# Which engine signals between score products, and the order of the first period, in an attention and MLP kernel

## The chip, the cores and the metric

The kernel runs on one core of one Trainium2 chip. The metric is the device time of one execution in microseconds (us), from the first to the last thing the device does for it; lower is better. Engines are named as in the profile: PE is TensorE (PEld its weight loads), DVE VectorE, ACT ScalarE, POOL GpSimd, SP SyncE. A name with a q behind it (SPq) is the instruction queue of that engine, which issues DMAs and handles semaphores in program order.

## The reference

Attention over 8 batches of 8 heads, 576 tokens and 64 dimensions, in which only scores within tau of their row's maximum keep a weight; its output, 4608 rows of 512, goes through two matrices with a leaky ReLU between them.

```python
scores = scale * np.matmul(q, k.transpose(0, 1, 3, 2))            # (8, 8, 576, 576)
thresh = np.max(scores, axis=-1, keepdims=True) - tau
scores = np.where(scores >= thresh, scores, -1e9)
scores = scores - np.max(scores, axis=-1, keepdims=True)
attn = np.exp(scores)
attn = attn / (np.sum(attn, axis=-1, keepdims=True) + 1e-09)
x = np.matmul(attn, v).transpose(0, 2, 1, 3).reshape(4608, 512)
h = x @ w_in                                                       # 512 x 2048
return np.maximum(0.01 * h, h) @ w_out                             # 2048 x 512
```

## The kernel before

The work is cut into 72 periods. A period holds 128 queries of four heads; the heads form two pairs, and the two heads of a pair are the two halves (h = 0 and 1) of the 128 rows of PE. So a period has four score tiles (c, h) of 128 x 576, with c the pair. The order of work in a period is written out by hand (the pools do no scheduling), and every engine runs its instructions in that order.

In each period `scores` issues 24 products into `sc`, a PSUM tile of five banks (L296). q and k are each split in two 16-bit parts, a high and a low one, so every piece of a tile takes three products: high with high, low q with high k, high q with low k. The two row halves run beside each other on PE. The four tiles lie in `sc` without gaps, each spans a bank's edge, and tiles of different halves share a bank. So the first product of piece a12 (half 0) must come behind the last product of piece b12 (half 1) of the same period. This order is made by a signal: an instruction without work (`nop`, L325) on another engine waits for b12, and PE waits for the signal ahead of a12. Before the change the signal is on ACT in periods 0 to 2, on POOL in 3 to 5 and on SP from period 6 on. As each queue runs in order, the signal also waits for what stands ahead of it in that queue, and holds up what stands behind it.

DVE then copies each tile out of PSUM with its row's minimum of the negated score (`copy_min`, L332), makes the threshold (L347), and multiplies the exponentials that ACT computes (L358) by the mask (L369), which gives the weights w; ACT does one or two of the tiles by itself (L363, L364). In periods 0 to 2 PE transposes the weights (L388, copied by ACT and DVE, L393); from period 3 on SP issues a DMA transpose into wT (`turn_w`, L380). Two periods later PE multiplies wT with v (`pv`, L417), DVE scales the result (L436), and layer 1 (L457, with ACT's L460) and layer 2 (L470) follow, spread over the periods.

Keys and queries come in by DMA and have to be transposed and split. For batch 0, and a few pieces of batch 1, PE transposes them in 32 bits (`turn32`, L211), ACT takes the high half (`take_high`, L232) and DVE the low half (`take_low`, L239). For the others POOL splits them (L160, L167, L171) and PE transposes both halves (L186). `k32[p]` are the keys of pair p of batch 0, `q32` its queries. Matmuls on a blank tile (`idle`, L514) fill PE in the first four periods.

The queues carry, beside the signals: SP the loads of q, k and v (L75, L86, L99, and L93, L106 for the tails of 64 tokens), the DMA transposes and the stores; POOL the splits, casts of v (L113), the loads of w_in and w_out (L123, L127, cast on the way), copies of the first keys (L253), and from period 5 on the loads of tails.

In period 0 PE's order is: the products of both pairs, the transposes of `k32[2]` and `q32[1, 0]`, 32 idle products, the transposes of `k32[3]`; then period 1. DVE's is: `take_low` of `k32[1]` (ahead of the loop), the copies of tiles 0, 1 and 2, `take_low` of `k32[2]`, the copy of tile 3, `take_low` of `q32[1, 0]`, the threshold, weights. The products of the second pair need the low half of `k32[1]`.

Of the kernel before, what the change touches and what calls it, by code (L numbers as in the profile page):

```python
# [33 lines left out]
def kernel(  # L34
# [10 lines left out]
    nc = tc.nc  # L45
# [128 lines left out]
    def turn(keys):  # L174

        banks = [ps.tile([128, 1024], FP16, tag="h", bufs=2, name="tp") for _ in range(2)][::-1]
        at_ = 0
        for key in keys:
            half, n = halves.pop(key), tokens(key)
            tps[key] = [t[:, ds(at_, 128 * n)].rearrange("d (x t p) -> d x t p", x=2, t=n) for t in banks]  # L180
            at_ += 128 * n
            for x in range(2):
                for t in range(n):
                    for r in range(2):
                        rows = ds(64 * r, 64)
                        nc.tensor.transpose(tps[key][r][:, x, t, :], half[rows, x, t, :, :].rearrange("p h d -> p (h d)"),  # L186
                                            ident[rows, rows])
        return banks[0]


    def unit32(b, which, p0, np=1, t0=0, nt=4):
        return (b, which, p0, np, t0, nt)
# [3 lines left out]
    def turn32(keys, tag="h"):  # L196
        bank = ps.tile([128, 512], FP32, tag=tag, bufs=2 if tag == "h" else 1, name="tp")
        c0 = 0
        for key in keys:
            b, which, p0, np, t0, nt = key  # L200
            n = 256 if p0 == "t" else 128 * np * nt
            tps32[key] = bank[:, ds(c0, n)]
            if p0 == "t":
                for t in range(2):
                    nc.tensor.transpose(bank[:, ds(c0 + 128 * t, 128)],
                                        tails[b, which][:, t, :, :].rearrange("p h d -> p (h d)"), ident32[:, :])
            else:
                for p in range(np):
                    for t in range(nt):
                        src = raws[b, (p0 + p) // 2, which][:, t0 + t, ds(2 * ((p0 + p) % 2), 2), :]  # L210
                        nc.tensor.transpose(bank[:, ds(c0 + 128 * (nt * p + t), 128)],  # L211
                                            src.rearrange("p h d -> p (h d)"), ident32[:, :])
            c0 += n

    def place32(key, x, i, parts):

        b, which, p0, np, t0, nt = key
        dst, tp = turned_of(b, which), tps32[key]
        if p0 == "t":
            c0 = MAIN if which == "q" else 0  # L220
            return dst[:, x, :, ds(c0, 64)].rearrange("d (u s) p -> d s u p", u=2)[:, i, :, :], \
                tp.rearrange("d (i u p) -> d i u p", i=2, p=64)[:, i, :, :]
        c0 = (64 if which == "k" else 0) + 128 * t0
        n = 128 * nt // parts
        return dst[:, x, ds(p0, np), ds(c0 + n * i, n)], \
            tp.rearrange("d (p c) -> d p c", p=np)[:, :, ds(n * i, n)]

    def take_high(keys, parts=1):
        for key in keys:
            for i in range(2 if key[2] == "t" else parts):  # L230
                dst, tp = place32(key, 0, i, parts)
                nc.scalar.activation(out=dst, in_=tp, func=AF.Copy, bias=0.0, scale=64.0)  # L232

    def take_low(keys, parts=1):
        for key in keys:
            for i in range(2 if key[2] == "t" else parts):
                dst, tp = place32(key, 1, i, parts)
                high, _ = place32(key, 0, i, parts)
                nc.vector.scalar_tensor_tensor(out=dst, in0=tp, scalar=64.0, in1=high, op0=AX.mult, op1=AX.subtract)  # L239
# [34 lines left out]
    def pieces(c, h):  # L274
        a = PLACE[c, h]
        cut = (a // 512 + 1) * 512
        return [(a, cut - a), (cut, a + 576 - cut)]

    HALVES = ((0, 0), (1, 0), (0, 1))

    BEHIND = mybir.DependencyInfo(mybir.DependencyClass.Sync, mybir.DependencyReason.DATA)

    def product(st, c, h, piece, i):
        a, n = piece
        qx, kx = HALVES[i]
        rows = ds(64 * h, 64)
        key0 = 64 * (1 - h) + a - PLACE[c, h]
        for u in range(2 if st.tail else 1):
            pair = 2 * c + u if st.tail else 2 * st.pp + c
            if st.tail:  # L290
                lhs = turned[st.b, "q"][rows, qx, pair, MAIN:S]
                o = sc[ds(64 * u, 64), ds(a, n)]
            else:
                lhs = turned[st.b, "q"][rows, qx, pair, ts(st.m, 128)]
                o = sc[:, ds(a, n)]
            yield nc.tensor.matmul(out=o, lhsT=lhs, rhs=turned[st.b, "k"][rows, kx, pair, ds(key0, n)],  # L296
                                   start=(i == 0), stop=(i == 2), skip_group_check=True)

    TILES = ((0, 0), (0, 1), (1, 0), (1, 1))

    def scores(st):

        st.mn = sb.tile([128, 4], FP32, tag="mn", bufs=2, name="mn")
        st.th = sb.tile([128, 4], FP32, tag="th", bufs=2, name="th")
        st.s, st.e = {}, {}
        (a00, a01), (b01, b00) = pieces(0, 0), pieces(0, 1)
        (a11, a12), (b12, b11) = pieces(1, 0), pieces(1, 1)
        todo = [[(0, a00), (0, a01), (1, a11), (1, a12)], [(1, b12), (1, b11), (0, b01), (0, b00)]]
        if st.n < 2:

            todo[1] = todo[1][2:] + todo[1][:2]
        todo = [[(c, x, i) for c, x in row for i in range(3)] for row in todo]
        at_, signal, first = [0, 0], None, None
        while todo[0] or todo[1]:
            h = 1 if not todo[0] or (todo[1] and at_[1] < at_[0]) else 0
            c, x, i = todo[h].pop(0)
            at_[h] += x[1]
            for mm in product(st, c, h, x, i):
                if first is not None:
                    tc.declare_no_dep(mm.ins, first.ins, reason="other banks")  # L320
                if (h, x) == (0, a12) and i == 0:
                    tc.add_manual_dep(mm.ins, signal.ins.name, BEHIND, reason="the row halves share a bank")
                last = mm
            if (h, x) == (1, b12) and i == 2:
                signal = (nc.scalar if st.n < 3 else nc.gpsimd if st.n < 6 else nc.sync).nop()  # L325
                tc.add_manual_dep(signal.ins, last.ins.name, BEHIND, reason="the row halves share a bank")
            if (h, x) == (0, a11) and i == 2:
                first = copy_min(st, 0)

    def copy_min(st, n):  # L330
        st.s[TILES[n]] = sb.tile([128, 576], FP32, tag=f"s{n}", bufs=1, name="s")
        return nc.vector.tensor_scalar(  # L332
            out=st.s[TILES[n]][:, :], in0=sc[:, ds(PLACE[TILES[n]], 576)], scalar1=-1.0 / UNIT, scalar2=None,
            op0=AX.mult, op1=AX.min, accum_out=st.mn[:, n : n + 1])

    def copies(st, before, taken, lows):
        taken()
        copy_min(st, 1)
        copy_min(st, 2)
        if lows:  # L340
            take_low(lows[0])
        copy_min(st, 3)
        for keys in lows[1:]:
            take_low(keys)
        if before:
            recip(before)
        nc.vector.tensor_scalar(out=st.th[:, :], in0=st.mn[:, :], scalar1=1.0, scalar2=tau_f, op0=AX.mult, op1=AX.add)  # L347
        st.w = sb.tile([128, 2, 9, 128], FP16, tag="w", bufs=3, name="w")
        st.sum = sb.tile([128, 2, 2], FP32, tag="sum", bufs=3, name="sum")
# [23 lines left out]
    def recip(st):  # L373
        st.rec = sb.tile([128, 2, 2], FP16, tag="rec", bufs=4, name="rec")
        with nc.allow_low_precision(reason="as the weights"):
            nc.vector.reciprocal(out=st.rec[:, :, :], in_=st.sum[:, :, :])
# [172 lines left out]
    k32 = [[unit32(0, "k", p)] for p in range(NP)]  # L549
# [13 lines left out]
    take_low([q32[0, 0]])  # L563
    turn32(k32[1], "o")
    take_high(k32[1])
    take_low(k32[1])
    early32[0] = [k32[2], [q32[1, 0]]]
    late32[0] = k32[3]
    early32[1] = [[q32[0, 1]]]
# [46 lines left out]
    n = 0  # L616
    while n < N + PV_LAG or l1q or pending or l2q or stores:
        st = periods[n] if n < N else None
# [4 lines left out]
        keys, now32, late = turns_at.get(n, []), early32.get(n, []), late32.get(n)  # L623


        if st:
            scores(st)
        bank = turn(keys) if keys else None
        for x in now32:
            turn32(x)  # L630
        if here:
            before.wt = sb.tile([128, 2, 9, 128], FP16, tag="wT", bufs=4, name="wT")
# [13 lines left out]
        if st:  # L646
            copies(st, before, lambda: [take(key, 1, on_dve) for key in keys], now32)
            exp_plain(st, 0)
        elif before:
            recip(before)  # L650
# [117 lines left out]
```

## Time and profile before

| | |
|---|---|
| Median of 3 runs | 486.68 us (486.44 to 487.24) |
| The profiled execution | 486.76 us |
| Its span, first to last instruction | 485.0 us |
| PE busy | 467.4 us, 96% of the span |
| DVE, ACT, POOL busy | 433.0, 419.5, 214.9 us |
| Mean granted clock of PE | 0.991 |

Times in the views are microseconds from the start of the span. A row of the timeline gives the start, the time covered, the engine, the line, the operation with its output and inputs, their shapes and the count; in brackets stand the idle time of the engine before it and what ended that. In a row of waits stand the waiting engine and line, whom it waited for, the total, how often, and the longest. In a row of a DMA queue stand packets, MB and the share of 16 engines' time; in a row of DMA issues the count, the KB of each and the time from issue to landing. The chain of waits follows the work back from the last instruction, and shows the piece of each step that counts.

### The profile page before, as it was taken

To read this page: it belongs to the slowest core of one execution; us is meant where nothing else is said; L and a number is where in the kernel's file an instruction comes from. 1 tells how busy PE (TensorE), PEld (TensorE's weight loads), DVE (VectorE), ACT (ScalarE), POOL (GpSimd) and SP (SyncE) were. 2 spreads that over 40 slices of the span, in tenths; PEclk is the share of its full clock that TensorE was granted. 3 is DMA by queue.
4 is the path that set the end of the run, shared out by engine and by line. 5 is a ranking of instruction groups with operands and counts; after the bars stand their busy time and mean duration, and the time that the engine had idled before them with its cause. 6 is when DMAs were issued, how large, how long until landed. Compare 5 with 4: busy or idle time off the path is not lost.

```text
span 485.0 us, 25242 instructions
## 1 busy us (share of the span) xinstructions
PE 467.4 (96%) x10858; PEld 379.5 (78%) x10858; DVE 433.0 (89%) x1313; ACT 419.5 (86%) x779; POOL 214.9 (44%) x353
## 2 busy tenths in 40 slices
PE   8779799999999999999999999999999999999996
PEld 5567688887888888887888888888888788777774
DVE  4988599999999999999999999999999999999940
ACT  3888588998999999999899999999999899988862
POOL 2645545554465574454456574455357464000000
PEclk9999799999999999999999999999999999999999
DMA  9999959699999989799799979698799979557851
GB/s 179 240 209 228 181 146 186 145 163 200 170 198 201 216 151 197 156 167 210 177 185 194 222 164 177 159 182 194 182 188 205 204 173 123 123 122 122 122 96 45
DMA packets 206752, 83.68 MB, mean 173 GB/s; under 512 B 175792, under 2 KB 201392, under 8 KB 206640
## 3 DMA queue, kind: packets, MB, share of 16 engines
q1 hardware_dynamic: 199728, 74.79, 79.1%
q0 software_dynamic: 5504, 6.82, 7.5%
q8 instruction: 85, 1.39, 1.2%
q10 hardware_dynamic: 1408, 0.46, 0.4%
q14 instruction: 27, 0.22, 0.1%
HBM read 36.70 MB, written 9.44 MB: 95 GB/s over the span
## 4 chain that ended last, share of the span: by engine, by line
PE 83%; DMA 6%; ACT 5%; DVE 2%; SPq 2%; issue 1%; ACTq 0%; DVEq 0%
PE hp L457 25%; PE o L470 24%; PE sc L296 20%; PE pv L417 8%; DMA wT<-w 5%; PE tp L401 3%; PE tp L186 3%; ACT e L358 1%; ACT wT L393 1%; SPq L86 1%; DMA raw<-in_k_dram 1%; ACT s L363 1%; DVE w L369 1%; ACT w L364 1%; ACT g L460 1%
## 5 line engine op out<-in xcount | busy, mean ns | idle before, releaser
L332 DVE TENSOR_SCALAR_CACHE_REDUCE s<-sc 128x576 f32<-128x576 f32 x288 | 205.4, 753 | 16.0 <-PE sc L296 15.7
L457 PEld LDWEIGHTS <-win 128*64 128x64 f16 x4608 | 147.1, 111 | 28.9 <-DVE xt L428 1.1
L369 DVE SCALAR_TENSOR_TENSOR w<-s,th,e 128x576 f16<-128x576 f32 x215 | 165.2, 814 | 0.4
L358 ACT ACTIVATE e<-s,mn 128x576 f16<-128x576 f32 x215 | 158.9, 777 | 0.0
L470 PE MATMUL o<-wout,g 128*64 128x512 f16 x1152 | 149.5, 381 | 0.0
L457 PE MATMUL hp<-x,win 128*64 128x128 f16 x4096 | 137.1, 220 | 0.3 <-DVE kT L249 0.3
L296 PE MATMUL sc<-kT,qT 64*128 64x384 f16 (+7 forms) x1920 | 120.7, 284 | 5.1 <-SPq L325 3.4
L460 ACT ACTIVATE g<-hp 128x512 f16<-128x512 f32 x144 | 86.1, 598 | 42.2 <-PE hp L457 42.2
L296 PEld LDWEIGHTS <-qT 64*128 64x128 f16 (+1 forms) x1920 | 90.0, 97 | 22.1 <-SPq L325 4.4
L160 POOL TENSOR_SCALAR scaled<-raw 128x512 f32<-128x512 f32 x53 | 32.7, 616 | 148.8 <-DVE w L369 139.0
L470 PEld LDWEIGHTS <-g 128*64 128x64 f16 x1152 | 58.6, 111 | 29.2 <-issue 0.5
L171 POOL TENSOR_TENSOR half<-scaled,half 128x512 f16<-128x512 f32 (+1 forms) x68 | 71.6, 1053 | 5.8
L364 ACT ACTIVATE w<-s,minus_tau 128x576 f16<-128x576 f32 x73 | 56.6, 775 | 2.4
L363 ACT ACTIVATE s<-s,th 128x576 f32<-128x576 f32 x73 | 56.0, 767 | 0.0
L417 PE MATMUL pv<-wT,v 128*64 128x128 f16 (+1 forms) x1600 | 53.5, 216 | 2.0 <-DMA wT<-w 1.1
L417 PEld LDWEIGHTS <-v 128*64 128x64 f16 x1600 | 46.1, 111 | 3.2 <-issue 1.4
L167 POOL CAST half<-scaled 128x512 f16<-128x512 f32 (+1 forms) x68 | 38.3, 563 | 4.4
L436 DVE TENSOR_TENSOR x<-pv,by 128x256 f16<-128x256 f32 x64 | 27.1, 423 | 8.8 <-PE pv L417 7.6
L407 ACT COPY by<-tp 128x256 f16<-128x256 f16 x72 | 26.8, 372 | 2.3 <-PE tp L388 2.3
L186 PEld LDWEIGHTS <-half 64*128 64x128 f16 x968 | 24.7, 96 | 2.3 <-issue 1.5
L186 PE MATMUL tp<-ident,half 64*128 64x64 f16 x968 | 24.5, 191 | 0.0
L113 POOL CAST v<-vraw 128x256 f16<-128x256 f32 x64 | 24.0, 408 | 0.0
(61 smaller groups left out, 336.8 us busy)
## 6 DMA issues: line engine op xcount, KB each, us to landing
vraw<-in_v_dram SPq DMA_DIRECT2D x16, 512.0 KB, 5.1
out_dram<-osb SPq DMA_DIRECT2D x31, 256.0 KB, 4.0
raw<-in_q_dram SPq DMA_DIRECT2D x13, 512.0 KB, 4.7
raw<-in_k_dram SPq DMA_DIRECT2D x13, 512.0 KB, 4.9
win<-in_moe_w_in_dram POOLq DMA_DIRECT2D x4, 512.0 KB, 11.5
wout<-in_moe_w_out_dram POOLq DMA_DIRECT2D x4, 512.0 KB, 15.0
raw<-in_q_dram SPq DMA_DIRECT2D x12, 128.0 KB, 3.9
raw<-in_k_dram SPq DMA_DIRECT2D x10, 128.0 KB, 4.1
```

Source lines behind the costliest of these rows:

```text
L171: nc.gpsimd.tensor_tensor(out=halves[key][:, 1, 0:n, :, :], in0=scaled.pop(key)[:, 0:n, :, :], in1=halves[key][:, 0, 0:n, :, :], op=AX.sub ...
L186: nc.tensor.transpose(tps[key][r][:, x, t, :], half[rows, x, t, :, :].rearrange("p h d -> p (h d)"), ident[rows, rows])
L296: yield nc.tensor.matmul(out=o, lhsT=lhs, rhs=turned[st.b, "k"][rows, kx, pair, ds(key0, n)], start=(i == 0), stop=(i == 2), skip_group_ch ...
L332: return nc.vector.tensor_scalar(out=st.s[TILES[n]][:, :], in0=sc[:, ds(PLACE[TILES[n]], 576)], scalar1=-1.0 / UNIT, scalar2=None, op0=AX. ...
L358: nc.scalar.activation(out=st.e[t][:, :], in_=st.s[t][:, :], func=AF.Exp, bias=st.mn[:, n : n + 1], scale=-1.0)
L363: nc.scalar.activation(out=z, in_=z, func=AF.Prelu, bias=st.th[:, n : n + 1], scale=-1.0, alpha=1e20)
L364: nc.scalar.activation(out=w_of(st, t), in_=z, func=AF.Exp, bias=minus_tau[:, :], scale=1.0, accum_out=st.sum[:, c, h : h + 1])
L369: st.last = nc.vector.scalar_tensor_tensor(out=w_of(st, t), in0=st.s[t][:, :], scalar=st.th[:, n : n + 1], in1=st.e[t][:, :], op0=AX.is_le ...
L417: nc.tensor.matmul(out=st.pv[ds(64 * h, 64), c, ts(u, n)], lhsT=v16[st.b % 2][:, pair, blk, :], rhs=st.wt[:, c, blk - (blk > 4), ts(u, n)] ...
L457: nc.tensor.matmul(out=hp[ds(64 * c, 64), jj, :], lhsT=w_in16[:, i, ds(128 * (4 * u + jj) + 64 * c, 64)], rhs=g.x[:, i, :], start=(i == 0) ...
L460: nc.scalar.activation(out=g.g[:, ds(4 * u, 4), :], in_=hp[:, :, :], func=AF.Prelu, bias=0.0, scale=1.0, alpha=0.01)
L470: nc.tensor.matmul(out=g.o[ds(64 * c, 64), :], lhsT=g.g[:, j, ds(64 * c, 64)], rhs=w_out16[:, j, :], start=(j == 0), stop=(j == 15), skip_ ...
```

## The change

It does two things. The signal of each period moves to another engine, by a list: POOL in period 0, ACT in 1, SP in 2, POOL in 3 to 8, SP from 9 on. So it changes in periods 0 and 2 (ACT before) and 6 to 8 (SP before).

And period 0 gets another order. All 12 products of pair 0 are issued first; then, before any product of pair 1, come the copies of tiles 0 and 1, `take_low` of `k32[1]` and the 32-bit transposes of `k32[2]` and `q32[1, 0]`. Then pair 1's 12 products follow, and `take_low` of `k32[2]` stands ahead of the copies of tiles 2 and 3. In the other periods the first copy is declared independent of the products issued after it; in period 0 this declaration falls away with the moved copy.

```diff
+    SIGNAL = [nc.gpsimd, nc.scalar, nc.sync] + [nc.gpsimd] * 6 + [nc.sync]
...
-    def scores(st):
+    def scores(st, between=None):
...
         while todo[0] or todo[1]:
+            if between and todo[0][0][0] == 1 and todo[1][0][0] == 1:
+                between()
+                between = None
             h = 1 if not todo[0] or (todo[1] and at_[1] < at_[0]) else 0
+            if between and todo[h][0][0] == 1:
+                h = 1 - h
             c, x, i = todo[h].pop(0)
...
-                signal = (nc.scalar if st.n < 3 else nc.gpsimd if st.n < 6 else nc.sync).nop()
+                signal = SIGNAL[min(st.n, 9)].nop()
                 tc.add_manual_dep(signal.ins, last.ins.name, BEHIND, reason="the row halves share a bank")
-            if (h, x) == (0, a11) and i == 2:
+            if (h, x) == (0, a11) and i == 2 and st.n:
                 first = copy_min(st, 0)
...
     def copies(st, before, taken, lows):
         taken()
-        copy_min(st, 1)
-        copy_min(st, 2)
+        if st.n:
+            copy_min(st, 1)
+            copy_min(st, 2)
         if lows:
             take_low(lows[0])
+        if not st.n:
+            copy_min(st, 2)
         copy_min(st, 3)
...
     take_high(k32[1])
-    take_low(k32[1])
...
-        if st:
+        if n == 0:
+            def between():
+                copy_min(st, 0)
+                copy_min(st, 1)
+                take_low(k32[1])
+                for x in now32:
+                    turn32(x)
+            scores(st, between)
+        elif st:
             scores(st)
         bank = turn(keys) if keys else None
-        for x in now32:
+        for x in now32 if n else []:
             turn32(x)
```

## The prediction

> **What bounds the kernel now.** I read the page first, busy time by engine:
>
> ```profile
> PE 467.4 (96%) x10858; PEld 379.5 (78%) x10858; DVE 433.0 (89%) x1313; ACT 419.5 (86%) x779; POOL 214.9 (44%) x353
> ```
>
> TensorE (PE) is busy for 96% of the span, so the span falls only by PE idle time, or by PE time at a low clock. Then the waits, for idle time that ends in a score signal. From 48 to 75 us:
>
> ```profile
> PE sc L296 <- SPq L325: 2.8, 1, 2.8
> ```
>
> One stall of PE, released by SyncE's queue (SPq) at L325, the score signal. The timeline of PE puts it in period 6:
>
> ```profile
> 50.08 1.32 PE L296 MATMUL sc<-kT,qT 64*128 64x384 f16 x19
> ```
>
> ```profile
> 54.19 0.82 PE L296 MATMUL sc<-kT,qT 64*128 64x256 f16 x5 [2.79 <-SPq L325]
> ```
>
> PE stops at 51.40 with 5 of 24 products left. The timeline of SP's queue shows why the signal is late:
>
> ```profile
> 47.80 3.33 SPq L380 DMA_TRANSPOSE wT<-w  x1
> 51.18 2.89 SPq L86 DMA_DIRECT2D raw<-in_q_dram  x4
> 54.33 3.37 SPq L380 DMA_TRANSPOSE wT<-w  x1
> ```
>
> The signal stands behind the transpose of period 4's weights (47.80) and four loads (51.18 to 54.07). It does no work; SP just isn't there. The stall also costs clock. Two stages of the windows view (length, busy time of PE, PEld, DVE, ACT, POOL, then the granted clock):
>
> ```profile
> 53.00:54.00 1.00, 0.00 (x0) 0.00 (x0) 0.00 (x0) 0.00 (x0) 0.92 (x2) 0.66 0.24 46
> ```
>
> ```profile
> 60.00:60.20 0.20, 0.20 (x10) 0.20 (x8) 0.00 (x0) 0.20 (x2) 0.07 (x1) 0.65 0.25 62
> ```
>
> If the clock is 1.0 or 0.5, a mean of 0.66 over 1 us puts the drop at 53.32 and 0.65 over 0.2 us puts the return at 60.06. So from 54.19 to 60.06 PE works at half rate: 5.87 us, half of it lost, 2.9 us. Stall and slow stretch together are 5.7 us, the most that this place can give.
>
> The other limit here is the transposed weights wT that the second product (pv, L417) reads two periods later:
>
> ```profile
> 38.12 5.93 SPq L380 DMA_TRANSPOSE wT<-w  x1
> ```
>
> ```profile
> 47.64 0.75 PE L417 MATMUL pv<-wT,v 128*64 128x128 f16 x20 [0.45 <-DMA wT<-w]
> ```
>
> wT of period 3 is issued at 38.12, and PE already waits 0.45 us for it at 47.64. The DMA view says what holds it. From 38 to 40 us, then from 42 to 44:
>
> ```profile
> q0 software_dynamic: 409, 0.41, 122.6%
> ```
>
> ```profile
> q1 hardware_dynamic: 749, 0.19, 99.2%
> q0 software_dynamic: 100, 0.09, 27.8%
> ```
>
> While q0 (GpSimd's weight loads) has work, q1 (SP's) moves nothing of the transpose; it moves as q0 drains. So this landing follows the end of the weight loads rather than the compute, and so does SP, whose issue takes 5.93 us here against 3.33 and 3.37 later.
>
> **Period 0.** Pair 0's 12 products stand in the same place. PE rows:
>
> ```profile
> 7.90 1.32 PE L296 MATMUL sc<-kT,qT 64*128 64x384 f16 x16
> 9.38 0.87 PE L296 MATMUL sc<-kT,qT 64*128 64x256 f16 x8 [0.16 <-DVE kT L239]
> 10.18 0.88 PE L211 MATMUL tp<-ident,raw 128*128 128x128 f32 x6
> 10.98 1.94 PE L514 MATMUL spare<-blank,ident 128*64 128x256 f16 x32
> 12.85 0.66 PE L211 MATMUL tp<-ident,raw 128*128 128x128 f32 x4
> ```
>
> Chain of waits, the take_low of k32[1] and the three copies (each with its accumulator):
>
> ```profile
> 8.63 0.70 DVE kT L239
> ```
>
> ```profile
> 9.73 2.12 DVE s L332 x6
> ```
>
> 12 of the 16 products take 12/16 of 1.32 = 0.99 us, so pair 0 ends at 8.89. Now two copies start at 8.92 instead of 9.73, at 2.12/3 = 0.71 each: they end at 10.34. That is a lead of 0.81 us. But in the built program PE's first product of pair 1 waits for the second copy, since nothing declares them independent any more; before, four of pair 1's products ran before any copy. PE fills the gap with the six transposes (0.88, 8.89 to 9.77) and waits to 10.38. Behind the copies stands take_low of k32[1], 10.34 to 11.04; the last eight products need it, 0.87 more: they end at 11.95, not 10.25. The 32 idle products queue behind them: they start at 11.95 instead of 10.98, and all that follows on PE is 0.97 later, the transposes of k32[3] at 13.82 too. From there ACT's and DVE's rows:
>
> ```profile
> 13.62 0.59 ACT L232 ACTIVATE kT<-tp 128x512 f16<-128x512 f32 x1
> ```
>
> ```profile
> 14.39 0.69 DVE L239 SCALAR_TENSOR_TENSOR kT<-tp,kT 128x512 f16<-128x512 f32 x1
> ```
>
> ACT's take_high goes from 13.62 to 13.82 + 0.66 + 0.02 = 14.50, DVE's take_low from 14.39 to 14.50 + 0.59 + 0.03 = 15.12. DVE's weights stand behind it: period 0 ends 0.7 us later, not earlier. From the other side, if pair 1 started as soon as pair 0 ended, about 0.8 us would be won, the lead of the first copy. I take +0.7, since the wait is there. The signal costs nothing: GpSimd's (POOL's) queue holds only the weight loads behind it, which wait for a load of v anyway.
>
> **Period 2.** The signal goes from ACT to SP. PE and ACT rows:
>
> ```profile
> 23.05 0.50 PE L296 MATMUL sc<-kT,qT 64*128 64x256 f16 x5 [1.12 <-ACTq L325]
> ```
>
> ```profile
> 22.98 0.78 ACT L364 ACTIVATE w<-s,minus_tau 128x576 f16<-128x576 f32 x1
> ```
>
> ```profile
> 23.99 0.50 PE L388 MATMUL tp<-ident,w 128*64 128x128 f16 x12
> ```
>
> The 1.12 us wait goes, but L388 transposes what this L364 writes, ready at 23.76 at the earliest: 0.23 us is all that can be won, and 0.1 is what I count. On SP the wait has a queue behind it:
>
> ```profile
> 16.88 1.06 SPq L75 DMA_DIRECT2D raw<-in_q_dram  x1
> 17.98 1.34 SPq L93 DMA_DIRECT2D rawt<-in_k_dram  x2
> ```
>
> ```profile
> raw<-in_q_dram SPq DMA_DIRECT2D x1, 512.0 KB, 10.4
> ```
>
> These loads (640 KB) now issue at about 22.7 to 25 instead of 16.88 to 19.32. With the same 10.4 us the first lands near 33; its reader:
>
> ```profile
> 38.15 0.62 POOL L160 TENSOR_SCALAR scaled<-raw 128x512 f32<-128x512 f32 x1 [3.72 <-PE sc L296]
> ```
>
> So 5 us of cover remain. The bytes move from one part of a full DMA stretch to another, so I leave the end of q0 where it is. If that is wrong, they lengthen it by 640 KB at 0.41 MB in 2 us = 3.1 us (third rival).
>
> **To period 6.** PE reaches pv of period 3 0.6 to 0.7 us later, at 47.19 + 0.7 = 47.89 instead of waiting to 47.64: 0.25 us lost, the rest is eaten by the 0.45 us wait. Scores of period 6 start at 50.33.
>
> **Periods 6 to 8.** POOL's queue at that time:
>
> ```profile
> 47.68 0.67 POOL L171 TENSOR_TENSOR half<-scaled,half 128x256 f16<-128x256 f32 x1
> ```
>
> It is free from 48.35 (+0.7) and its next work waits for DVE, so the 2.79 us stall goes, and with it the half clock. Undisturbed, period 7 shows how long PE needs:
>
> ```profile
> 62.07 1.64 PE L296 MATMUL sc<-kT,qT 64*128 64x384 f16 x24
> 63.55 0.40 PE L186 MATMUL tp<-ident,half 64*128 64x64 f16 x16
> ```
>
> ```profile
> 65.86 0.66 PE L211 MATMUL tp<-ident,raw 128*128 128x128 f32 x4
> 66.62 0.75 PE L417 MATMUL pv<-wT,v 128*64 128x128 f16 x20
> 67.18 0.63 PE L470 MATMUL o<-wout,g 128*64 128x512 f16 x4
> ```
>
> From the scores to the end of layer 1: 65.86 - 62.07 = 3.79, and 0.20 for the 8 more transposes of period 6 (half of 0.40). PE is ready for pv of period 4 at 50.33 + 3.99 = 54.32. What is late next is wT of period 4, issued at 47.80. Its time to landing, in the DMA view:
>
> ```profile
> wT<-w SPq DMA_TRANSPOSE x1, 7.6
> ```
>
> It lands at 55.40, so PE waits 1.1 us, pv runs at 55.44 and layer 2 follows 67.18 - 66.62 = 0.56 later, at 56.00. Before:
>
> ```profile
> 59.20 1.18 PE L417 MATMUL pv<-wT,v 128*64 128x128 f16 x20
> 60.21 0.60 PE L470 MATMUL o<-wout,g 128*64 128x512 f16 x4
> ```
>
> 60.21 - 56.00 = 4.2 us. The next wT, if it takes as long, lands at 54.33 + 7.6 = 61.9, ahead of its pv at 66.62 - 4.2 = 62.4. From there PE is busy nearly throughout, so the lead stays. In periods 7 and 8 SP's signal stalled nobody, so POOL can only lose. Its worst place is period 7:
>
> ```profile
> 57.52 2.55 POOL L93 DMA_DIRECT2D rawt<-in_q_dram  x4
> ```
>
> These four issues end at 60.07; they hang on period 6's transposes, which move some 3 us ahead, so they end near 57 to 58, while the signal is wanted about 1.2 us after the scores of period 7 start at 57.8. I count 0, at worst 1 us.
>
> **Sum.** 0.25 us are lost by period 5, 5.7 us go in period 6, and 1.1 us of new wait come in, which by the start times of layer 2 leaves 4.2 (the three would leave 4.35; pv at half rate and its follower differ by the rest). The profiled execution took 486.76 us, of which 1.8 lie around the span, where nothing changes; the median is 486.68. Less 4.2: 482.5.
>
> **A rule weighed.** The clock fell here after 51.40 to 53.32, 1.9 us without a matmul, in a gap of 2.79 us; the 1.12 us gap at 22 us left it whole. My new gap (54.32 to 55.44) is like the latter, so I charge no clock. The Trainium skill (TensorE: Matmul & The Clock Gate, section "Why this matters for your kernels") allows idle gaps up to about 3 us; by that rule the 2.79 us gap would not have dropped the clock, and the sum by it would be the fourth rival's, 485.5. The trace speaks against it: the drop falls inside the gap.
>
> **Rivals.** First, wT of period 4 follows the 0.7 us of the start (SP's 5.93 us are its own, not the backlog's): landing 56.1, gain 3.5, 483.2. The rows with q1 still speak against it: 20%. Second, that transpose lands sooner and PE doesn't wait: pv at 54.32, gain 60.21 - 54.88 = 5.3, 481.4 (481.2 without the 0.25 us lost at the start); 7%. Third, slower: the moved loads push q0's end out by 3.1 us. Then pv of period 3 runs at 50.74 after a gap of 2.85 us, the clock falls at 47.89 + 1.92 = 49.81 for 6.74 us, to 56.55; of the 6.43 us of work to the next pv (54.32 - 47.89) 2.9 are done by then, so that pv comes at 60.1, layer 2 at 60.6 to 60.7: 0.4 us slower, 487.1, and each further us costs one. It decides from about 2.7 us. Against it: the sum of bytes is the same. 10%. Fourth, the half clock comes back whatever the gap: 2.9 us of the gain go and 1.3 stay, 485.5; 6%. Fifth, it doesn't do what it says: another wait stands at the same place and PE resumes no sooner, 486.7; 3%, since PE's wait there names SP's signal alone.
>
> **How the numbers follow.** The forecast has 54%. About 0.2%, 1 us, is what a measurement here tells from none. Faster: 54 + 20 + 7 and 5 of the fourth's 6 = 86%. Same: 1 of it, the fifth's 3 and 3 of the third's 10 = 7%; slower: the third's other 7%. The range goes from the second rival (481.2) to the fourth (485.5); it leaves out the third and the fifth, 13%.
>
> **What would show it.** After: no idle of PE released by a score signal in period 6, clock 1.00 from 50 to 60 us, a wait of about 1 us for wT ahead of pv of period 4; period 0's products ending near 12 us, period 3's pv near 47.9. A gap over 2 us at 47 or 54 us, or clock 0.5 anywhere there, makes it wrong.

## The result and the profile after

The changed kernel takes 484.45 us (median of 6 runs, 482.94 to 485.46), the kernel before 486.69 us (6 runs beside it, 486.15 to 488.23). The ratio is 0.9946, with a 95% interval of 0.9924 to 0.9967: 2.6 us faster (1.6 to 3.7), where 4.2 were forecast. The profiled execution after took 482.94 us, with a span of 481.2 us; before, it was 486.76 and 485.0. In this pair of executions the span fell by 3.8 us.

All lines below the change have moved: score products L296 to L297, the signal L325 to L331, the transposes of the weights L380 to L389 (by DMA) and L388 to L397 (by PE), pv L417 to L426, layer 2 L470 to L479.

The timeline of PE after: period 6's score products, pv of period 4 with the layer 2 behind it, and pv of period 5:

```profile
51.09 1.65 PE L297 MATMUL sc<-kT,qT 64*128 64x384 f16 x24
55.84 0.75 PE L426 MATMUL pv<-wT,v 128*64 128x128 f16 x20 [0.75 <-DMA wT<-w]
56.40 1.06 PE L479 MATMUL o<-wout,g 128*64 128x512 f16 x8
62.84 0.75 PE L426 MATMUL pv<-wT,v 128*64 128x128 f16 x20
```

Period 6's 24 products run in one piece, without the stall of 2.79 us. Ahead of pv of period 4 there is a new wait, for wT. Layer 2 follows at 56.40 instead of 60.21: 3.81 us earlier, which is all that the span fell by. The same two windows as before, where the clock had been 0.66 and 0.65:

```profile
53.00:54.00 1.00, 1.00 (x18) 0.48 (x12) 1.00 (x5) 1.00 (x4) 0.94 (x2) 1.00 1.10 253
60.00:60.20 0.20, 0.20 (x16) 0.15 (x10) 0.20 (x1) 0.20 (x1) 0.14 (x2) 1.00 0.70 155
```

The clock (the number behind POOL's count) is whole. SP's queue, from the timeline, and the piece of the chain of waits that ends at the new wait:

```profile
39.48 5.56 SPq L389 DMA_TRANSPOSE wT<-w  x1
48.77 3.30 SPq L389 DMA_TRANSPOSE wT<-w  x1
52.13 2.87 SPq L86 DMA_DIRECT2D raw<-in_q_dram  x4
55.17 2.92 SPq L389 DMA_TRANSPOSE wT<-w  x1
```

```profile
48.77 6.93 DMA wT<-w
```

The four loads at 52.13 are still in SP's queue while PE multiplies, but no signal stands behind them any more. The transpose of period 4's weights is issued 0.97 us later than before and lands 0.30 us later, at 55.70.

The start of the kernel, first after, then the one row of before that isn't shown yet:

```profile
8.52 1.21 PE L297 MATMUL sc<-kT,qT 64*128 64x384 f16 x12
9.65 0.87 PE L211 MATMUL tp<-ident,raw 128*128 128x128 f32 x6
11.27 0.44 PE L297 MATMUL sc<-kT,qT 64*128 64x320 f16 x4 [0.74 <-ACT qT L232]
18.08 0.53 PE L397 MATMUL tp<-ident,w 128*64 128x128 f16 x12 [0.24 <-DVE w L378]
```

```profile
16.61 0.53 PE L388 MATMUL tp<-ident,w 128*64 128x128 f16 x12 [0.24 <-DVE w L369]
```

Pair 0's products, the six transposes and then a gap ahead of pair 1's first products: the shape that the prediction drew. The row names ACT's `take_high` (done at 11.22) for the gap's end; DVE's second copy, which the prediction named, is done at 11.21, and in e3's profile the same gap of 0.74 us is put down to it. This execution begins 0.62 us later (8.52 against 7.90; the first loads of keys landed later), so of the 1.47 us between 16.61 and 18.08, 0.85 belong to the new order. Period 2, where the signal went to SP:

```profile
22.09 1.64 PE L297 MATMUL sc<-kT,qT 64*128 64x384 f16 x24
25.37 0.47 PE L397 MATMUL tp<-ident,w 128*64 128x128 f16 x9 [0.93 <-ACT w L373]
```

The products are in one piece here too, and PE waits for ACT's weights right behind them: 25.84 is 1.35 us behind the 24.49 of before, where the period had begun 1.48 us behind. So 0.13 us are won.

### The profile page after: what moved, and what is told of

The parts are those of the page before. It is cut to its first block, busy times and chain, and to the rows that moved or that the text cites. A ratio compares the mean times of both kernels' runs of the same rounds, so it can differ in the third digit from the quotient of the medians.

```text
span 481.2 us, 25242 instructions
## 1 busy us (share of the span) xinstructions
PE 465.2 (97%) x10858; PEld 378.2 (79%) x10858; DVE 433.4 (90%) x1313; ACT 419.8 (87%) x779; POOL 214.9 (45%) x353
## 3 DMA queue, kind: packets, MB, share of 16 engines
q0 software_dynamic: 5504, 6.82, 7.6%
## 4 chain that ended last, share of the span: by engine, by line
PE 83%; DMA 7%; ACT 6%; DVE 2%; issue 1%; SPq 0%; ACTq 0%
PE hp L466 24%; PE o L479 24%; PE sc L297 20%; PE pv L426 8%; DMA wT<-w 6%; PE tp L410 3%; PE tp L186 3%; ACT wT L402 1%; ACT w L373 1%; ACT e L367 1%; DMA raw<-in_k_dram 1%; ACT s L372 1%; DVE w L378 1%; ACT g L469 1%; DVE s L338 0%
## 5 line engine op out<-in xcount | busy, mean ns | idle before, releaser
L479 PE MATMUL o<-wout,g 128*64 128x512 f16 x1152 | 148.8, 379 | 0.0
L297 PE MATMUL sc<-kT,qT 64*128 64x384 f16 (+7 forms) x1920 | 120.1, 284 | 1.2 <-ACT qT L232 0.7
L297 PEld LDWEIGHTS <-qT 64*128 64x128 f16 (+1 forms) x1920 | 89.9, 97 | 17.9 <-issue 1.1
L479 PEld LDWEIGHTS <-g 128*64 128x64 f16 x1152 | 58.7, 110 | 28.6 <-ACT g L469 0.3
L426 PE MATMUL pv<-wT,v 128*64 128x128 f16 (+1 forms) x1600 | 53.1, 214 | 2.8 <-DMA wT<-w 1.8
L426 PEld LDWEIGHTS <-v 128*64 128x64 f16 x1600 | 45.7, 110 | 4.0 <-PE hp L466 2.3
L338 DVE DVE_READ_ACCUMULATOR s<-sc 128x1 f32 x288 | 24.0, 83 | 0.0
```

The costliest lines, as they stand in the source:

```text
L338: return nc.vector.tensor_scalar(out=st.s[TILES[n]][:, :], in0=sc[:, ds(PLACE[TILES[n]], 576)], scalar1=-1.0 / UNIT, scalar2=None, op0=AX. ...
L426: nc.tensor.matmul(out=st.pv[ds(64 * h, 64), c, ts(u, n)], lhsT=v16[st.b % 2][:, pair, blk, :], rhs=st.wt[:, c, blk - (blk > 4), ts(u, n)] ...
L479: nc.tensor.matmul(out=g.o[ds(64 * c, 64), :], lhsT=g.g[:, j, ds(64 * c, 64)], rhs=w_out16[:, j, :], start=(j == 0), stop=(j == 15), skip_ ...
```

## The experiments

Theory: the gain is all in period 6, by the stall and the clock, and what is left of it is set by the landing of the weights' transposes. Rivals: the new order of period 0 or the signal of period 2 does something for the time; the clock is worth more, or less, than was counted; what the transposes wait for is SP's order.

Ratios are to the kernel before on the same chip, with 95% intervals. The kernels of each group ran on one chip: e1 to e4 beside 35 runs of before with a median of 487.46 us, e5 to e8 beside 35 with 486.44, e9 to e11 beside 22 with 486.43, e12 beside 17 with 485.85.

**e1: the change once more.** No edit.

> The changed kernel once more. Theory A (the gain is the stall and the half clock of period 6, less a new wait for the transposed weights of period 4): 3.8 us less than before in an execution that loads its first keys as early as before did, clock 1.00 from 50 to 60 us, PE waiting about 0.8 us for wT ahead of pv of period 4. Rival B (the gain itself varies: the period 0 order makes the start sensitive): the trace of this execution shows a longer wait for wT than 0.8 us, or another stall in the first 60 us, and a gain nearer 2 us.

484.78 us (12 runs, 482.52 to 486.46), ratio 0.9948 (0.9925 to 0.9970): 2.5 us faster (1.5 to 3.7), where 3.8 were expected. The result holds, but this profiled execution is another one than the first: 486.46 us, span 484.6. PE, and the windows of 2 us around it:

```profile
57.19 0.84 PE L426 MATMUL pv<-wT,v 128*64 128x128 f16 x20 [2.31 <-DMA wT<-w]
```

```profile
56.00:58.00 2.00, 0.81 (x22) 0.84 (x24) 0.43 (x1) 1.26 (x2) 2.00 (x4) 0.93 1.34 233
58.00:60.00 2.00, 2.00 (x20) 1.25 (x16) 1.87 (x6) 0.00 (x0) 0.89 (x2) 0.50 1.39 200
60.00:62.00 2.00, 2.00 (x39) 1.84 (x37) 0.77 (x4) 0.61 (x2) 0.01 (x1) 0.72 1.30 145
```

The wait for the same transpose is 2.31 us here, and half clock follows. With a clock of 1.0 or 0.5, its length is twice the missing share of each window: 2 x (0.07 + 0.50 + 0.28) x 2.00 = 3.4 us. So the new wait is not of one size, and it can bring the old loss back.

**e2: the signal of periods 6 to 8 alone.** The order of period 0 and the signals of 0 and 2 stay as before.

```diff
-                signal = (nc.scalar if st.n < 3 else nc.gpsimd if st.n < 6 else nc.sync).nop()
+                signal = (nc.scalar if st.n < 3 else nc.gpsimd if st.n < 9 else nc.sync).nop()
```

> Only the signals of periods 6 to 8 go to POOL; periods 0 to 5 and the order of period 0 stay as before. Theory A: all of the gain is here. Scores of period 6 start as before (50.1), PE is ready for pv of period 4 at 54.1, wT lands at about 55.4, so layer 2 follows at 56.0: 4.2 us less than before, 482.5, and 0.4 to 1 us less than the changed kernel. Rival B (period 0's order and period 2's signal carry part of the gain): less than 3 us here.

484.27 us (482.55 to 486.57), ratio 0.9945 (0.9922 to 0.9968), 2.7 us faster (1.6 to 3.8). That is less than the 4.2 expected, and less than the 3 us set as the mark for rival B. But the changed kernel gains no more than this, so this one edit is the whole gain. Its two waits, for wT of periods 4 and 5:

```profile
55.11 0.75 PE L417 MATMUL pv<-wT,v 128*64 128x128 f16 x20 [0.79 <-DMA wT<-w]
62.95 0.75 PE L417 MATMUL pv<-wT,v 128*64 128x128 f16 x20 [0.95 <-DMA wT<-w]
```

**e3: the new order of period 0 alone.** The changed kernel with the signals as before.

```diff
-                signal = SIGNAL[min(st.n, 9)].nop()
+                signal = (nc.scalar if st.n < 3 else nc.gpsimd if st.n < 6 else nc.sync).nop()
```

> Only the order of period 0 changes; all signals stay as before. Theory A: products of period 0 end about 1.7 us later, idle products 1.0 us later, the weights of period 0 0.7 to 0.9 us later; PE's wait of 0.45 us for wT of period 3 swallows part; the stall of period 6 remains, since SP's queue is as late or up to 1 us later: 0 to 1 us slower than before, 486.7 to 487.7. Rival (the reorder helps): 0.5 us or more faster.

487.41 us (484.88 to 491.1), ratio 1.0002 (0.9974 to 1.0029): no difference that shows in 12 runs. The stall of period 6 is there, and half clock after it, of 3.4 us by the same reckoning:

```profile
55.27 0.50 PE L297 MATMUL sc<-kT,qT 64*128 64x256 f16 x5 [2.60 <-SPq L331]
```

```profile
54.00:56.00 2.00, 0.73 (x25) 0.71 (x27) 0.00 (x0) 0.00 (x0) 1.92 (x4) 0.94 0.83 178
56.00:58.00 2.00, 2.00 (x24) 1.10 (x20) 1.64 (x5) 1.29 (x4) 0.67 (x2) 0.50 1.04 203
58.00:60.00 2.00, 2.00 (x52) 1.84 (x50) 1.21 (x6) 1.26 (x3) 2.00 (x4) 0.71 0.98 190
```

**e4: the stall stays, the clock is kept.** The kernel before; 40 blank products fill PE's wait in period 6.

```diff
             at_[h] += x[1]
+            if st.n == 6 and (h, x, i) == (0, a12, 0):
+                idle(20, spare("h"))
```

> As before, but in period 6 40 extra products on a blank tile (about 2.4 us) stand on PE ahead of the product that waits for SP's signal: the wait stays, the idle gap behind it shrinks to under 1 us. If the gap causes the half clock: clock 1.00 from 53 to 60 us, PE resumes at 54.2 at full rate, pv of period 4 near 57.0 and layer 2 near 57.6: 2.6 us less than before, 484.1. If the half clock comes whatever the gap (fourth rival): clock 0.5 again for some 6 us, and 0 us gained or some lost.

486.39 us (484.17 to 488.46), ratio 0.9971 (0.9944 to 0.9998): 1.4 us gained (0.1 to 2.7), where 2.6 were expected. PE and a window:

```profile
52.39 2.37 PE L516 MATMUL spare<-blank,ident 128*64 128x256 f16 x40
55.15 0.50 PE L296 MATMUL sc<-kT,qT 64*128 64x256 f16 x5 [0.39 <-SPq L327]
```

```profile
56.00:58.00 2.00, 2.00 (x52) 1.58 (x54) 1.96 (x7) 1.73 (x5) 0.91 (x3) 1.00 1.07 207
```

The wait for the signal is as long as ever, but PE works through it and the clock stays at 1.00. The clock term of the sum is real, and by the middle of the interval about half of what was counted.

**e5, e6, e7: two loads moved from SP to GpSimd.** In e2's profile the weights of period 4 are ready at 44.98, and their transpose is issued at 48.03 behind two loads of value tails (L106). The same edit in e2's kernel (e5), in the kernel before (e6) and in the changed kernel (e7):

```diff
-        if n >= 5:
+        if n >= 4:
             for f in small_at.get(n, []):
                 f(small=nc.gpsimd)
...
-        for f in loads_at.get(n, []) + (small_at.get(n, []) if n < 5 else []):
+        for f in loads_at.get(n, []) + (small_at.get(n, []) if n < 4 else []):
```

> The kernel before with the signal of periods 6 to 8 on GpSimd, and period 4's two loads of value tails (L106, 2.29 us of SP at 45.56) issued by GpSimd too. Theory: what is left of the gain is set by SP's order: the weights of period 4 are ready at 44.98 and their transpose is issued at 48.03, behind these loads. Then the transpose issues near 45.7 and lands near 53; PE's wait for it (0.79 us in the profile without this edit, 2.31 us in another) is gone, with it the occasional half clock; the wait of 0.95 us at 62.95 goes too, as that transpose moves up with the queue. Expected 482.3 to 483.3, against 484.3 without the edit, and a narrower spread. Rival: the landing is bound by the transfers on the DMA engines, so that the transpose issued earlier takes as much longer: 484.3, the wait stays within 0.5 us of what it was.

> The kernel before with period 4's two loads of value tails issued by GpSimd; the signal stays on SP. Theory: SP's queue is the resource, and the signal is only what stood last in it: its four loads of period 6 end near 51.7 instead of 54.07, the products of period 6 wait 0.4 us or less at their usual place (from 51.4), no half clock, and the weights of period 4 land in time: 482.3 to 483.5, as good as the change or better. Rival: the signal itself on SP is slow, whatever stands ahead of it: a stall of over 1 us stays and the time is 485.5 to 487.

> The changed kernel with the same two loads on GpSimd. Theory: the weights' transpose of period 4 no longer binds, so all of the gain shows, less what the new order of period 0 costs if that reaches the end: pv of period 3 waits for a transpose that was issued behind the loads, so at most 0.3 us of the start's 0.85 us get through: 482.3 to 483.6. Rival: the start's delay was hidden only behind the late transposes, and now shows whole: 0.9 us above the kernel with the signal of 6 to 8 and the loads moved.

All three missed. e5: 488.32 us (484.14 to 491.02), ratio 1.0033 (1.0004 to 1.0062), slower than before. e6: 487.67 us (486.58 to 489.39), ratio 1.0029 (1.0007 to 1.0051). e7: 484.16 us (481.55 to 485.86), ratio 0.9943 (0.9919 to 0.9967), no better than the change itself. In e5, GpSimd's queue and SP's, then PE, and what the DMA view has of the two landings between 38 and 44 us:

```profile
41.02 1.33 POOL L106 DMA_DIRECT2D vrawt<-in_v_dram  x2
```

```profile
38.51 7.46 SPq L380 DMA_TRANSPOSE wT<-w  x1
```

```profile
54.25 1.28 PE L417 MATMUL pv<-wT,v 128*64 128x128 f16 x20 [6.67 <-DMA wT<-w]
```

```profile
vrawt<-in_v_dram POOLq DMA_DIRECT2D x2, 64.0 KB, 11.3
wT<-w SPq DMA_TRANSPOSE x1, 15.7
```

GpSimd reaches the loads at 41.02, SP had issued them from 45.32 on in the kernel before. The transpose of period 3's weights, in flight then, takes 15.7 us instead of 9.5 in the kernel before. From 44 to 46 us SP's queue moved, before and in e5:

```profile
q1 hardware_dynamic: 1643, 0.49, 106.0%
```

```profile
q1 hardware_dynamic: 380, 0.10, 127.4%
```

More time of the DMA engines for a fifth of the bytes. In e6 the same wait is 3.23 us (pv at 50.47); the signal's stall has shrunk to 0.53 us, as the theory said, and the loss at pv ate it. In e7, with the same loads at 41.76, that transpose landed in 8.3 us and nothing was lost. So the two loads don't always do it, and what decides is not settled. What is shown: SP's order is not all that sets these landings.

**e8: SP in period 2 alone.**

```diff
-                signal = (nc.scalar if st.n < 3 else nc.gpsimd if st.n < 6 else nc.sync).nop()
+                signal = (nc.scalar if st.n < 2 else nc.sync if st.n == 2 else nc.gpsimd if st.n < 6 else nc.sync).nop()
```

> The kernel before with the signal of period 2 alone on SP (ACT in 0 and 1). Theory: products of period 2 end 0.2 us earlier at most and PE then waits for ACT's weights; no change within 0.5 us of the kernel before. Rival: SP's wait at the signal holds back its loads of period 3 and the transposes behind them, 0.5 to 1.5 us slower.

486.28 us (485.03 to 488.83), ratio 1.0002 (0.9977 to 1.0028). PE's wait goes to ACT's weights, as after, and the stall of period 6 is untouched:

```profile
24.33 0.47 PE L388 MATMUL tp<-ident,w 128*64 128x128 f16 x9 [0.93 <-ACT w L364]
```

```profile
54.38 0.82 PE L296 MATMUL sc<-kT,qT 64*128 64x256 f16 x5 [2.66 <-SPq L325]
```

**e9, e10: the two loads behind the transpose, still on SP.** In e2's kernel (e9) and in the changed kernel (e10):

```diff
-        at(small_at, v_at[2], lambda b=b, small=nc.sync: load_vtails(b, small=small))
+        if b == 1:
+            at(loads_at, 5, lambda b=b: load_vtails(b))
+        else:
+            at(small_at, v_at[2], lambda b=b, small=nc.sync: load_vtails(b, small=small))
```

> The kernel before with the signal of periods 6 to 8 on GpSimd, and period 4's two loads of value tails issued by SP in period 5, behind the transpose of period 4's weights instead of ahead of it; nothing goes to GpSimd's queue of loads. Theory A (order on SP): the transpose issues at 45.6 instead of 48.0 and, beside 1 MB of loads as the one before it, takes up to 9.5 us: it lands at 53 to 55, PE's wait ahead of period 4's second product (0.79 us without this edit) is 0.5 us or less, 483.2 to 484.0 against 484.3. Theory B (the transpose's landing is set by what else the DMA engines carry): it is issued earlier into more traffic, takes over 10 us and lands where it did or later, 484.3 or up to 2 us more, with some runs at a lower clock.

> The changed kernel with the same two loads behind the transpose. By theory A the wait for the transpose of period 4 (0.75 us in the first profile, 2.31 us in the second) is 0.5 us or less: 483.0 to 484.0. By theory B 484.5 or more.

e9: 486.12 us (483.54 to 489.61), ratio 0.9989 (0.9964 to 1.0014). e10: 485.08 us (483.05 to 487.94), ratio 0.9971 (0.9944 to 0.9999). PE, pv of periods 4 and 5, e9 and then e10:

```profile
54.24 0.75 PE L417 MATMUL pv<-wT,v 128*64 128x128 f16 x20
64.57 1.28 PE L417 MATMUL pv<-wT,v 128*64 128x128 f16 x20 [3.37 <-DMA wT<-w]
```

```profile
54.74 0.72 PE L426 MATMUL pv<-wT,v 128*64 128x128 f16 x20
62.85 0.75 PE L426 MATMUL pv<-wT,v 128*64 128x128 f16 x20 [1.00 <-DMA wT<-w]
```

Both times miss what theory A gave and lie where theory B put them. For period 4's wait theory A is right: its transpose, issued at 45.59 in e9, lands in time and the wait is gone. But the next transpose is late then, and in e9's execution by so much that half clock follows. The wait has moved one period on.

**e11: the kernel before once more.**

> The kernel before, unchanged, once more. The size of the clock's loss: if the 6.74 us at half clock behind the stall of period 6 is what this stall costs, they are here again (mean clock 0.991 to 0.993). If it was two stretches of about 3.4 us by chance, one of them is here (0.995 to 0.996) and the loss is 1.7 us or less, or none.

487.04 us in its one run; span 485.3 us, mean clock 0.994. PE's stall and the windows:

```profile
55.34 0.50 PE L296 MATMUL sc<-kT,qT 64*128 64x256 f16 x5 [3.40 <-SPq L325]
```

```profile
56.00:58.00 2.00, 2.00 (x30) 1.05 (x24) 1.77 (x5) 1.54 (x4) 0.62 (x2) 0.60 1.29 181
58.00:60.00 2.00, 2.00 (x47) 2.00 (x44) 1.26 (x6) 0.98 (x3) 2.00 (x4) 0.55 1.11 244
```

A longer stall than the first (3.40 us) and half as much half clock: 2 x (0.40 + 0.45) x 2.00 = 3.4 us. What the prediction read as 6.74 us were two such stretches.

**e12: the two loads in period 6, behind both transposes.** As e10, with `at(loads_at, 6, ...)`.

> The changed kernel with the two loads of value tails issued by SP in period 6, behind the transposes of both period 4's and period 5's weights. The weights of period 5 are ready at 53.36 in the changed kernel's profile, SP's four loads before it end at 54.0, so that transpose issues near 54.0 (55.56 with the loads in period 5) and lands near 61.4 at the 7.4 us of its issue, 62.9 at the longest landing so far (8.9). Theory: both waits (period 4's and 5's second product) are 0.5 us or less in sum, the time is 482.8 to 484, below the changed kernel's 484.5 by up to 1.7 us. Rival: each transpose moved ahead only runs beside more traffic and the next one is late instead (period 6's, by over 1 us): 484.5 to 486.

483.8 us (482.68 to 486.64), ratio 0.9950 (0.9928 to 0.9972): as good as the change (0.9946 and 0.9948), not better. pv of periods 4 and 5:

```profile
54.79 0.75 PE L426 MATMUL pv<-wT,v 128*64 128x128 f16 x20
63.12 0.75 PE L426 MATMUL pv<-wT,v 128*64 128x128 f16 x20 [1.35 <-DMA wT<-w]
```

Half of the theory holds: period 4's wait is gone and none of the 12 runs has a mean clock below 0.998. But period 5's second product starts at 63.12, and in the other profiles without half clock at nearly the same time: 62.84 (changed kernel), 62.95 (e2), 63.35 (e7) and 62.85 (e10). In e12 its transpose is issued at 54.80, 0.37 us earlier than in the changed kernel (55.17), but takes 8.3 us to land instead of 7.2, so that PE waits for it. In the changed kernel PE comes to it at 62.84 by its own work, without a wait. So what period 4 won is lost again in period 5. None of the kernels beats the change by more than its interval.

## Why the prediction was right, and where its sum was too large

The direction, the mechanism and the range held. Step by step:

- **Period 0: +0.97 us on PE, +0.7 us behind it.** Right. From pair 0's first product to the first transposed weights, the eight profiles with the old order have 8.71 to 8.78 us (8.71 before), the six with the new one 9.38 to 9.83 (9.56 after): 0.88 us longer in the mean. That only 0.25 us get through to pv of period 3 fits (48.65 without a wait, against 47.64 behind a wait of 0.45; less the 0.62 us of late first loads, 0.39), and e3's interval, 1.4 us to either side, can't tell it from nothing.
- **Period 2: 0.1 us won.** 0.13 us in the profile, and nothing measurable in e8. The moved loads (issued from 22.77 on) did not push out the end of q0: from 42 to 44 us it has 0.10 MB left to move in e8, as in the kernel before (0.25 MB in the profile after, which had the late start), and pv of period 3 waits for nothing. So the third rival, the slower one, did not come.
- **Period 6: the stall of 2.79 us goes.** Right, and e2 shows that this alone is the gain. The stall was of typical size: 2.66 (e8), 2.60 (e3) and 3.40 us (e11).
- **The clock: 2.9 us.** This term failed. It was read from one execution, and its half clock was taken for the price of the stall. (A slip in it is small: a mean of 0.65 over 0.2 us puts the clock's return at 60.14, not 60.06, so the half clock lasts 6.82 us.) The profiles show stretches of one length, 3.4 us: one in e1, e3, e6, e8 and e11, two in the first profile, e5 and e9, none in the others. The mean clock of a run tells how many there were: profiles with 0.991 to 0.993 have two, with 0.994 to 0.996 one, with 0.999 or 1.0 none. Of 108 runs of before beside the experiments (without one of 493.71 us), 35 have 0.998 or more, 64 have 0.994 to 0.996 and 9 have 0.993 or less: (64 + 2 x 9)/108 = 0.76 stretches each, at 3.4/2 = 1.7 us at most, 1.3 us. The times of these runs agree: in the four sets, the median of those with one stretch is 0.7 to 1.4 us above that of those with none. Of the changed kernel's 18 runs 2 have one, 0.2 us. So the clock brings 1.1 us at most, not 2.9; e4 measures 1.4 us for it (0.1 to 2.7).
- **The new wait: 1.1 us.** About right in size, wrong in being one number: 0.75 and 2.31 us in the two profiles of the changed kernel, 0.79 us in e2. In the execution with 2.31 us a gap over 2 us and a clock of 0.5 stand at the place that the prediction named as proof against it; it is the rarer case. The first rival is partly true too: SP's issue of the transposes did move with the start (48.77 against 47.80), though its landing gave most of that back.
- **Periods 7 and 8: 0.** Right: no wait for GpSimd's signal shows on PE.

With these sizes the sum is: a stall of 2.9 us (mean of 2.79, 3.40, 2.66 and 2.60) less a wait of 1.3 (mean of 0.75, 2.31 and 0.79), 1.6; clock 1.1; start -0.3, taken between the 0.25 forecast and the 0.39 seen: 2.4 us, an estimate from a few profiles. Measured: 2.6 (1.6 to 3.7) and in e1 2.5 (1.5 to 3.7). The pair of profiled executions lay at 3.8 us mainly because the one before had two stretches of half clock and the one after had none.

The rule that was weighed stays refuted as to the gap: gaps of 2.31, 2.60, 2.66 and 2.79 us were followed by half clock, those up to 1.50 us (at 28.83 in the kernel before) were not. Another statement of the Trainium skill (TensorE: Matmul & The Clock Gate, Part 1) fits better: there the clock is decided in free-running windows of 3413 ns. The trace agrees on the length, 3.4 us or twice that each time. By the Trainium skill's table in that part the default, half clock, comes back after a whole idle window; here 2.31 us of idle time were enough.

Open is what spreads the runs of the changed kernel over 482.5 to 486.3 us where their clock is whole. The later waits for transposes in the profiles differ by up to 1 us between executions, which is not all of it.

## What to carry to other kernels

Before a loss is priced from one profiled execution, look whether its mean clock is that of the median run: here the profiled one had 0.991 where the median run had 0.996, and the price was more than twice too high. A signal that does no work belongs on a queue that is empty when it is due; moving it for three periods was worth the whole gain. And when a stall is taken out, the next transfer in line sets the end: its landing varies from run to run, and moving what stands ahead of it in the queue only made the one behind it late.

## What the hardware showed that was not expected

Half clock comes in pieces of one length. Summed from windows of 0.4 us, the stretches behind gaps of PE are 3.41 to 3.42 us (gaps of 2.31, 2.60, 2.66, 3.23 and 3.40 us, in e1, e3, e8, e6 and e11) or 6.82 to 6.83 us (gaps of 2.79, 3.37 and 6.67 us, in the first profile, e9 and e5). They don't begin at a fixed time in the gap: 0.87 us before PE resumes in the first profile, 0.49 us after it in e3 (55.76 against 55.27), 0.53 us after it in e1 (57.72 against 57.19). A longer gap did not always mean more half clock.

What fits all eight profiles is how much of the gap falls into one window of this length. Lay a grid of 3.41 us through the fall of the clock in each of them, from 10 us to 470. Of over 1000 windows at full clock, the eight in which PE idled 1.91 to 3.39 us were followed by half clock, and none with 1.50 us or less was. After a window at half clock the next was at half clock too when PE had idled 0.87, 1.37 or 3.27 us in it, and at full clock when it had idled 0.59 us or less. In the kernel before, and in e8, length, busy time of PE, PEld, DVE, ACT and POOL, then the clock:

```profile
49.90:53.31 3.41, 1.50 (x29) 1.03 (x23) 2.52 (x7) 2.13 (x4) 1.33 (x3) 1.00 1.40 143
53.31:56.72 3.41, 2.54 (x39) 1.83 (x41) 1.03 (x3) 0.68 (x2) 1.73 (x3) 0.50 1.13 193
56.72:60.14 3.42, 3.42 (x56) 2.93 (x54) 1.82 (x8) 2.31 (x6) 3.11 (x5) 0.50 0.96 182
```

```profile
50.38:53.79 3.41, 1.34 (x23) 0.95 (x19) 2.36 (x7) 2.13 (x4) 1.49 (x3) 1.00 0.86 194
53.79:57.20 3.41, 2.81 (x39) 1.94 (x41) 1.31 (x5) 0.96 (x3) 1.60 (x4) 0.50 0.95 190
57.20:60.62 3.42, 3.42 (x96) 2.86 (x92) 2.97 (x10) 3.26 (x6) 3.07 (x5) 1.00 0.67 143
```

Read so, the 2.79 us gap of before cost two stretches since 0.87 us of it fell into the second window, and the 2.66 us gap of e8 cost one, with 0.59 us there. The grid is fitted to these profiles, and no run tested it. An estimate from it: a gap of 2.8 us that falls at random on such a grid has less than 1.9 us in either window in (2 x 1.9 - 2.8)/3.41 = 29% of cases; 35 of the 108 runs of before, 32%, kept their clock.

Two small loads of 64 KB, issued by GpSimd some 4 us earlier, came with a much later landing of a transpose in flight on SP's queue (15.7 us in e5 and 12.3 us in e6 instead of 9.5), and in the changed kernel with none (8.3 us in e7).
